# A gated state-space and feed-forward kernel: output bias seeded in PSUM, the last 64 GELU features of two token tiles multiplied in the two row halves of TensorE

## The chip, the cores and the metric

The kernel runs on one core of one Trainium2 chip. The metric is the device time of one execution in microseconds (us), less is better. Each kernel was timed several times beside the kernel before, on the same chip. All runs quoted here were classed as undisturbed ("fast"). The granted clock is the share of the full TensorE clock that the chip allowed, as the profile records it; where its mean over a run was below 0.995, the text says so.

## The reference, cut to what matters

For 2048 tokens of 640 features, a diagonal complex state-space layer (a scan over time) and a two-layer feed-forward network with 1728 hidden features read the same x and are mixed by a per-token gate.

```python
def _B_ref(x, w1, b1, w2, b2):
    h = jnp.einsum("bsd,df->bsf", x, w1) + b1
    h = _gelu(h)
    return jnp.einsum("bsf,fd->bsd", h, w2) + b2      # w2: 1728 x 640

x = A_x
g = _sigmoid((x * gate_w).sum(-1, keepdims=True))
a = _A_ref(x, ...)      # scan, then 2 Re(h C^T) + x * Dskip
b = _B_ref(x, B_w1, B_b1, B_w2, B_b2)
return g * a + (1 - g) * b
```

1728 is 13 x 128 + 64. The sum over the hidden features needs 13 matmuls of 128 rows and one of 64. In the 64-row matmul half of the TensorE array has nothing to do.

## The kernel before

The tokens are worked in 4 chunks of 512, each of 4 tiles of 128. Per chunk there are four TensorE stages: `ssm` (input projection of the scan), `ff1` (first layer and GELU), `fin_b` (second layer) and `fin_a` (output projection of the scan). In the timelines below ScalarE works in the order in which the program issues to it. The program takes all its PSUM banks from one pool of eight.

```python
def last_tile(c, p, pv):            # the last 64 hidden features, and the gate
    # ... 20 small matmuls into one bank
    nc.scalar.activation(out=gelN[c % 2][:, :, 0:F_LAST], in_=pv[:, :, 0:F_LAST], func=ACT.Gelu_apprx_tanh)
    # ... then transposed by DMA into gel[c][:, KF - 1, :]

def fold(ks):                       # folds a complex factor into C, once
    nc.scalar.activation(out=t1[:], in_=CT_im[:, ks, :], func=ACT.Identity, scale=n2im[:, ks:ks + 1])
    nc.scalar.activation(out=t2[:], in_=CT_re[:, ks, :], func=ACT.Identity, scale=n2im[:, ks:ks + 1])
    # ... two VectorE operations

def fin_b(c):
    for a in range(TPC):                                    # 4 token tiles
        # ...
        for d0, d1 in HALVES:                               # 2 x 320 output features
            p = bank()
            for kf in range(KF):                            # 14
                m = P if kf < KF - 1 else F_LAST + 1        # 128, at last 65
                nc.tensor.matmul(p[:, 0:d1 - d0], lhsT=gel[c][:m, kf, lo:lo + P], rhs=w2_sb[:m, kf, d0:d1],
                                 start=(kf == 0), stop=(kf == KF - 1))
            nc.scalar.activation(out=gb[:, d0:d1], in_=p[:, 0:d1 - d0], func=ACT.Identity, scale=gcol[:, 1, ti:ti + 1])

# order at the first chunk
ssm(1)
gates(1)
for ks in range(KS):
    fold(ks)
fin_b(0)
fin_a(0)
```

Row 65 of the last matmul is a row of ones against `b2`, so the output bias needs no instruction of its own.

Of the kernel before, what the change touches and what calls it, by code (L numbers as in the profile page):

```python
# [11 lines left out]
ACT = mybir.ActivationFunctionType  # L12
BF16 = mybir.dt.bfloat16
F32 = mybir.dt.float32
I32 = mybir.dt.int32

P = 128
T = 2048
D = 640
F = 1728  # L20
CH = 512
NCH = T // CH
KD = D // P
KS = D // P
KF = (F + P - 1) // P
F_LAST = F - (KF - 1) * P
NT = T // P
TPC = CH // P
HD = D // 2
# [9 lines left out]
def kernel(  # L39
# [19 lines left out]
    nc = tc.nc  # L59
# [4 lines left out]
    const = ctx.enter_context(tc.tile_pool(name="const", bufs=1))  # L64
# [4 lines left out]
    work = ctx.enter_context(tc.tile_pool(name="work", bufs=2))  # L69
    fwork = ctx.enter_context(tc.tile_pool(name="fwork", bufs=5))  # L70

    def bank(dtype=F32):
        return ps.tile([P, CH * 4 // (4 if dtype == F32 else 2)], dtype, name="bank")
# [7 lines left out]
    w2_sb = const.tile([P, KF, D], BF16, name="w2_sb")  # L81
# [9 lines left out]
    prmB = const.tile([NB, P], BF16, name="prmB")  # L91
    colA = const.tile([P, 3 * KS], F32, name="colA")
    colB = const.tile([P, NB], F32, name="colB")
    Dbc = const.tile([P, D], BF16, name="Dbc")
    glast = const.tile([P, 2, KS], F32, name="glast")
    carry = const.tile([P, 2, KS], F32, name="carry")
    b1x = const.tile([P, F_LAST + 1], BF16, name="b1x")
    gelN = [const.tile([P, TPC, P], BF16, name=f"gelN{i}") for i in range(2)]
    gz = const.tile([P, NT], F32, name="gz")
    gcol = const.tile([P, 2, NT], F32, name="gcol")  # L100
# [28 lines left out]
    HC = CH // 4  # L129
# [1 line left out]
    nc.gpsimd.iota(tfi[:], pattern=[[1, HC]], base=0, channel_multiplier=0)  # L131
    nc.gpsimd.memset(b1x[:, F_LAST:F_LAST + 1], 0.0)
    for i in range(2):
        nc.gpsimd.memset(gelN[i][:, :, F_LAST:P], 0.0)
        nc.gpsimd.memset(gelN[i][:, :, F_LAST:F_LAST + 1], 1.0)
    nc.scalar.dma_start(out=prmB[KS:NB, :], in_=B_b1[0:(KF - 1) * P].rearrange("(j p) -> j p", p=P))
    nc.scalar.dma_start(out=prmB[0:KS, :], in_=gate_w.rearrange("(j p) -> j p", p=P))
    nc.sync.dma_start(out=b1x[:, 0:F_LAST], in_=B_b1[F - F_LAST:F].rearrange("(o d) -> o d", o=1).to_broadcast([P, F_LAST]))  # L138
# [4 lines left out]
    nc.sync.dma_start_transpose(out=CT_im[:], in_=A_C_im[:, :])  # L143
    nc.sync.dma_start(out=w2_sb[:, 0:KF - 1, :], in_=B_w2[0:(KF - 1) * P, :].rearrange("(kf p) d -> p kf d", p=P))
    nc.sync.dma_start(out=w2_sb[:F_LAST, KF - 1, :], in_=B_w2[(KF - 1) * P:F, :])
    nc.sync.dma_start(out=w2_sb[F_LAST:F_LAST + 1, KF - 1, :], in_=B_b2.rearrange("(o d) -> o d", o=1))
    nc.sync.dma_start(out=Dbc[:], in_=A_Dskip.rearrange("(o d) -> o d", o=1).to_broadcast([P, D]))
    nc.sync.dma_start_transpose(out=xT[2][:], in_=x2d[2 * CH:3 * CH, :])
    nc.sync.dma_start_transpose(out=xT[3][:], in_=x2d[3 * CH:4 * CH, :])
# [6 lines left out]
    class Clock:  # L156
        pe = 5.0
        act = 13.0
# [23 lines left out]
    def pe(cols):  # L182
        ck.pe += cols / 2400.0 + 0.002

    def act(cost):
        ck.act = max(ck.act, ck.pe + 0.2) + cost
        return ck.act
# [18 lines left out]
    def col(name, dtype=F32, n=KS):  # L206
        return const.tile([P, n], dtype, name=name)
# [37 lines left out]
    absq = col("absq", n=NQ * KS)  # L245
    sq = col("sq", n=NQ * KS)
    cq = col("cq", n=NQ * KS)
    kk = work.tile([P, KS, HC], I32, name="bu", bufs=8)

    def over(c):  # L250
        return c.rearrange("p (k o) -> p k o", o=1).to_broadcast([P, KS, HC])
# [11 lines left out]
    gel = [None] * NCH  # L263
    gbs = [None] * NT
# [5 lines left out]
    def ff1_act(p, c, kf):  # L270
        nc.scalar.activation(out=gel[c][:, kf, :], in_=p[:, :], func=ACT.Gelu_apprx_tanh, bias=b1_c[:, kf:kf + 1])  # L271
        act(0.69)
# [5 lines left out]
    def last_bank(c):  # L278
        p = bank()
        pv = p[:, 0:TPC * NL].rearrange("p (a n) -> p a n", a=TPC)  # L280
        if c == 0:
            nc.tensor.matmul(pv, lhsT=ident[:], rhs=b1x[:].rearrange("p (o n) -> p o n", o=1).to_broadcast([P, TPC, NL]),
                             start=True, stop=True, skip_group_check=True)
            return p, pv
        nc.scalar.activation(out=pv, in_=b1x[:].rearrange("p (o n) -> p o n", o=1).to_broadcast([P, TPC, NL]), func=ACT.Identity)
        act(0.4)
        return p, pv

    def last_tile(c, p, pv):
        for a in range(TPC):  # L290
            for kd in range(KD):
                nc.tensor.matmul(p[:, a * NL:(a + 1) * NL], lhsT=xT[c][:, kd, a * P:(a + 1) * P],  # L292
                                 rhs=w1b[kd][:, n1b - NL:n1b], start=False, stop=(kd == KD - 1), skip_group_check=True)
                pe(76)
        nc.scalar.activation(out=gelN[c % 2][:, :, 0:F_LAST], in_=pv[:, :, 0:F_LAST], func=ACT.Gelu_apprx_tanh)
        act(0.45)
        nc.scalar.activation(out=gz[:, c * TPC:(c + 1) * TPC], in_=pv[:, :, F_LAST:NL].rearrange("p a o -> p (a o)"), func=ACT.Tanh, scale=0.5)
        act(0.2)
        nc.sync.dma_start_transpose(out=gel[c][:, KF - 1, :].rearrange("p (a t) -> p a t", a=TPC),
                                    in_=gelN[c % 2][:].rearrange("p a n -> p (a n)"))  # L300

    def ff1(c, k0=0):
        for kf in range(k0, KF - 1):
            p = bank()
            if kf == KF - 3:
                last = last_bank(c)
            for kd in range(KD):
                ff1_mm(p, c, kf, kd)
            ff1_act(p, c, kf)
            let_out(ck.pe)  # L310
        last_tile(c, *last)
        let_out(ck.pe)
# [38 lines left out]
    lo, hi = slice(0, HC), slice(HC, HB)  # L351
# [119 lines left out]
    def ssm(c):  # L471
        hs[c] = hsp.tile([P, 2 * KS, CH], BF16, name="hs")
        for ks in range(KS):
            bu = work.tile([P, 2, CH], BF16, name="bu", bufs=8)
            for ri, BT in enumerate((BT_re, BT_im)):
                p = bank()
                for kd in range(KD):
                    nc.tensor.matmul(p[:], lhsT=BT[:, kd, ks * P:(ks + 1) * P], rhs=xT[c][:, kd, :],  # L478
                                     start=(kd == 0), stop=(kd == KD - 1))
                    pe(CH)  # L480
                nc.scalar.activation(out=bu[:, ri, :], in_=p[:], func=ACT.Identity)  # L481
                act(0.6)
            scan_ops(c, ks, bu, ck.act)
            if c == 0 and ks == 0:
                later(0, 1.6, factors)
            let_out(ck.pe)
# [12 lines left out]
    HALVES = ((0, HD), (HD, D))  # L499
    seeded = {}  # L500

    def cuts(ti):
        return ((0, HD), (HD, 512), (512, D)) if ti == NT - 1 else HALVES

    def seed(ti):

        c, a = divmod(ti, TPC)
        seeded[ti] = []
        for d0, d1 in cuts(ti):
            p = bank()  # L510
            dve_now(ck.pe, 0.45, lambda: nc.vector.tensor_tensor(out=p[:, 0:d1 - d0], in0=xn[c][:, a, d0:d1], in1=Dbc[:, d0:d1], op=ALU.mult))  # L511
            seeded[ti].append(p)

    def fin_b(c):
        for a in range(TPC):
            ti = c * TPC + a
            lo = a * P
            gb = fwork.tile([P, D], F32, name="gb")
            if a >= TPC - 2:
                seed(c * TPC + a - (TPC - 2))  # L520
            for d0, d1 in HALVES:
                p = bank()
                for kf in range(KF):
                    m = P if kf < KF - 1 else F_LAST + 1
                    nc.tensor.matmul(p[:, 0:d1 - d0], lhsT=gel[c][:m, kf, lo:lo + P], rhs=w2_sb[:m, kf, d0:d1],  # L525
                                     start=(kf == 0), stop=(kf == KF - 1))
                    pe(d1 - d0)
                nc.scalar.activation(out=gb[:, d0:d1], in_=p[:, 0:d1 - d0], func=ACT.Identity, scale=gcol[:, 1, ti:ti + 1])  # L528
                act(0.5)
            gbs[ti] = gb  # L530
            let_out(ck.pe)

    def fin_a(c):
        for a in range(TPC):
            ti = c * TPC + a
            lo = a * P
            ot = fwork.tile([P, D], BF16, name="ot", bufs=3)
            if a < TPC - 2:
                seed(ti + 2)
            for i, (d0, d1) in enumerate(cuts(ti)):  # L540
                p = seeded[ti][i]
                for j in range(2 * KS):
                    CT = CT_re if j < KS else CT_im
                    nc.tensor.matmul(p[:, 0:d1 - d0], lhsT=hs[c][:, j, lo:lo + P], rhs=CT[:, j % KS, d0:d1],  # L544
                                     start=False, stop=(j == 2 * KS - 1), skip_group_check=True)
                    pe(d1 - d0)

                def f():
                    nc.vector.scalar_tensor_tensor(out=ot[:, d0:d1], in0=p[:, 0:d1 - d0], scalar=gcol[:, 0, ti:ti + 1],  # L549
                                                   in1=gbs[ti][:, d0:d1], op0=ALU.mult, op1=ALU.add)  # L550

                dve_now(ck.pe + 0.2, 0.45, f)
                if ti == NT - 1 and i > 0:
                    s0 = 0 if i == 1 else d0
                    q = nc.sync if i == 1 else nc.scalar
                    q.dma_start(out=out2d[ti * P:(ti + 1) * P, s0:d1], in_=ot[:, s0:d1])
            if ti < NT - 1:
                nc.sync.dma_start(out=out2d[ti * P:(ti + 1) * P, :], in_=ot[:])
# [58 lines left out]
```

## Time and profile before

218.0 us is the median of the first three runs (217.83 to 218.4).

| what | value | where it is read |
|---|---|---|
| TensorE busy | 211.9 of 216.2 us | page, part 1 |
| VectorE, ScalarE busy | 88%, 42% | page, part 1 |
| chain of waits | DMA to 22.5 us, then TensorE alone to 213.2 us | chain |
| one `fin_b` stage | 112 matmuls, 15.24 us | chain |
| one matmul over 320 columns, start to start | 136 ns for 128 rows and for 65 | single records |

Here are lines of the chain of waits of the kernel before (start in us, length in us, what ran; a piece starts where the one before it ended, which is up to 0.2 us after its first matmul started). L525 is `fin_b`, L544 `fin_a`, L478 `ssm`.

```profile
22.49 9.89 PE bank L478 x45
...
57.81 15.25 PE bank L525 x112
73.06 10.87 PE bank L544 x80
...
109.36 15.24 PE bank L525 x112
```

After 22.5 us each piece starts where the last one ended, and all are TensorE. A nanosecond saved on TensorE is saved in the time, and a wait of TensorE is lost in full.

The groups by form show the two kinds of second-layer matmul and the seed of the last first-layer bank (line, engine, operation, tiles, shapes, count; then busy us, mean ns of one, idle before).

```profile
L525 PE MATMUL bank<-w_sb,gel 128*128 128x320 bf16 x416 | 61.1, 299 | 0.0
L525 PE MATMUL bank<-w_sb,gel 65*128 65x320 bf16 x32 | 9.6, 301 | 0.0
L285 ACT ACTIVATE bank<-b1x 128x260 f32<-128x260 bf16 x3 | 1.1, 383 | 0.0
```

299 ns is the length of one pipelined matmul, not its cost: the starts are 136 ns apart. The 65-row matmul is no cheaper, so 32 x 0.136 = 4.35 us go to work that fills half the array.

The last lines are ScalarE's timeline at the first `fin_b` (an eviction is the ScalarE operation that moves a finished bank to SBUF). The first is the last eviction of `ssm`, then come the first and the last of the ten fold operations, then evictions of `fin_b`.

```profile
57.85 0.60 ACT L481 ACTIVATE bu<-bank 128x512 bf16<-128x512 f32 x1 [0.48 <-PE bank L478]
58.34 0.82 ACT L397 ACTIVATE gb<-CT_im,n2im 128x640 f32<-128x640 bf16 x1
...
64.81 0.82 ACT L399 ACTIVATE gb<-CT_re,n2im 128x640 f32<-128x640 bf16 x1
65.53 2.42 ACT L528 ACTIVATE gb<-bank,gcol 128x320 f32<-128x320 f32 x5
```

The fold holds ScalarE from 58.3 to 65.5 us, while TensorE is already in `fin_b`. Before the change this held up nothing that mattered: the first evictions only came late, there were banks enough, and the chain shows TensorE going on without a stall.

### The profile page before, as it was taken

How to read it: one execution, taken by the hardware profiler on the slowest of the kernel's cores; microseconds unless marked ns; L12 is line 12 of the kernel's file. 1: busy time of each engine (PE TensorE's matmuls, PEld its weight loads, DVE VectorE, ACT ScalarE, POOL GpSimd, SP SyncE). 2: the span in 40 equal slices, each digit the busy share in tenths (PEclk: the TensorE clock that was granted, in tenths of full speed). 3: DMA queues.
4: the chain of work that ended last, by engine and by line, in shares of the span. 5: the costliest groups of instructions: out<-in, count | busy, mean ns of one | idle time of the engine just before them, and what ended most of it. 6: DMA issues, size and time to landing. Idle time of an engine off the chain costs nothing.

```text
span 216.2 us, 3470 instructions
## 1 busy us (share of the span) xinstructions
PE 211.9 (98%) x1368; PEld 128.2 (59%) x1368; DVE 189.8 (88%) x393; ACT 91.7 (42%) x156; POOL 1.6 (1%) x12
## 2 busy tenths in 40 slices
PE   7999999999999999999999999999999999999994
PEld 3855444454577775444477777444457777777773
DVE  3889999999999899999999999999999999961152
ACT  3689456675696101556642200456662210022100
POOL 2000000000000000000000000000000000000000
PEclk9999999999999999999999999999999999999999
DMA  5999999995000042000010006100001000100011
GB/s 174 255 224 199 226 214 369 175 246 103 3 0 0 0 141 106 0 0 3 0 24 3 0 0 200 45 2 0 0 3 24 0 3 30 61 30 3 2 61 61
DMA packets 32339, 16.16 MB, mean 75 GB/s; under 512 B 25091, under 2 KB 32324, under 8 KB 32324
## 3 DMA queue, kind: packets, MB, share of 16 engines
q1 hardware_dynamic: 32114, 15.91, 30.2%
q8 instruction: 10, 0.16, 0.3%
q10 hardware_dynamic: 210, 0.04, 0.1%
q14 instruction: 5, 0.04, 0.1%
HBM read 7.24 MB, written 2.62 MB: 46 GB/s over the span
## 4 chain that ended last, share of the span: by engine, by line
PE 88%; SPq 5%; DMA 5%; issue 0%; DVE 0%
PE bank L525 28%; PE bank L544 20%; PE bank L478 20%; PE bank L267 19%; DMA BT_im<-in_A_B_im_dram 3%; SPq L139 3%; DMA xn<-in_A_x_dram 1%; SPq L127 1%; SPq L125 1%; PE bank L292 1%; SPq L124 0%; SPq L138 0%; DVE ot L549 0%
## 5 line engine op out<-in xcount | busy, mean ns | idle before, releaser
L525 PE MATMUL bank<-w_sb,gel 128*128 128x320 bf16 x448 | 61.6, 299 | 0.0
L525 PEld LDWEIGHTS <-gel 128*128 128x128 bf16 x448 | 43.6, 98 | 17.2
L481 ACT ACTIVATE bu<-bank 128x512 bf16<-128x512 f32 x40 | 23.9, 597 | 41.7 <-PE bank L478 41.7
L271 ACT ACTIVATE gel<-bank,colB 128x512 bf16<-128x512 f32 x52 | 34.6, 693 | 15.1 <-PE bank L267 14.8
L544 PEld LDWEIGHTS <-hs 128*128 128x128 bf16 x330 | 31.8, 98 | 11.9
L434 DVE TENSOR_TENSOR_SCAN g<-r_c,carry,v 128x512 bf16<-128x512 f32 x30 | 37.2, 1270 | 0.0
L528 ACT ACTIVATE gb<-bank,gcol 128x320 f32<-128x320 f32 x32 | 16.5, 527 | 48.2 <-PE bank L525 46.6
L267 PE MATMUL bank<-xT,w1b 128*128 128x512 bf16 x140 | 31.0, 379 | 0.0
L267 PE MATMUL bank<-xT,w1a 128*128 128x512 bf16 (+1 forms) x150 | 27.6, 344 | 0.0
L544 PE MATMUL bank<-CT_im,hs 128*128 128x320 bf16 (+2 forms) x165 | 27.1, 295 | 0.0
L544 PE MATMUL bank<-CT_re,hs 128*128 128x320 bf16 (+2 forms) x165 | 27.1, 295 | 0.0
L549 DVE SCALAR_TENSOR_TENSOR ot<-bank,gcol,gb 128x320 bf16<-128x320 f32 (+2 forms) x33 | 17.3, 533 | 9.5 <-PE bank L544 9.3
L478 PE MATMUL bank<-xT,BT_im 128*128 128x512 bf16 x100 | 24.9, 379 | 0.1
L478 PE MATMUL bank<-xT,BT_re 128*128 128x512 bf16 x100 | 24.8, 379 | 0.0
L267 PEld LDWEIGHTS <-w1b 128*128 128x128 bf16 x140 | 13.6, 98 | 16.3 <-DMA w1b<-in_B_w_dram 0.3
L267 PEld LDWEIGHTS <-w1a 128*128 128x128 bf16 x150 | 14.9, 100 | 11.7
L511 DVE TENSOR_TENSOR bank<-xn,Dbc 128x320 f32<-128x320 bf16 (+2 forms) x33 | 14.3, 483 | 5.8 <-ACT gb L528 5.8
L478 PEld LDWEIGHTS <-BT_im 128*128 128x128 bf16 x100 | 9.7, 98 | 12.2 <-DMA BT_im<-in_A_B_im_dram 0.6
L478 PEld LDWEIGHTS <-BT_re 128*128 128x128 bf16 x100 | 9.7, 98 | 11.0
L415 DVE TENSOR_TENSOR v<-wa,wb 128x512 bf16<-128x512 bf16 x40 | 15.2, 421 | 0.7
L415 DVE TENSOR_TENSOR wa<-TCOS,g 128x1024 bf16<-128x1024 bf16 x20 | 13.7, 686 | 0.1
L415 DVE TENSOR_TENSOR wb<-TSIN,g 128x1024 bf16<-128x1024 bf16 x20 | 13.7, 684 | 0.0
(98 smaller groups left out, 130.7 us busy)
## 6 DMA issues: line engine op xcount, KB each, us to landing
out_dram<-ot SPq DMA_DIRECT2D x15, 160.0 KB, 1.8
w_sb<-in_B_w_dram SPq DMA_DIRECT2D x1, 2080.0 KB
xn<-in_A_x_dram SPq DMA_DIRECT2D x3, 640.0 KB, 4.9
w1b<-in_B_w_dram SPq DMA_DIRECT2D x5, 240.0 KB, 4.2
w1a<-in_B_w_dram SPq DMA_DIRECT2D x5, 192.0 KB, 3.5
xn<-in_A_x_dram SPq DMA_DIRECT2D x2, 320.0 KB
Dbc<-in_A_Dskip_dram SPq DMA_DIRECT2D x1, 160.0 KB
out_dram<-ot SPq DMA_DIRECT2D x1, 128.0 KB
```

The lines of the kernel that those rows point to most:

```text
L139: nc.sync.dma_start_transpose(out=BT_re[:], in_=A_B_re[:, :])
L267: nc.tensor.matmul(p[:, t0:t1], lhsT=w, rhs=xT[c][:, kd, t0:t1], start=(kd == 0), stop=(kd == KD - 1))
L271: nc.scalar.activation(out=gel[c][:, kf, :], in_=p[:, :], func=ACT.Gelu_apprx_tanh, bias=b1_c[:, kf:kf + 1])
L415: nc.vector.tensor_tensor(out=o, in0=a, in1=b, op=op)
L434: nc.vector.tensor_tensor_scan(s["g"][:, ri, :], r_c[:, ks:ks + 1].to_broadcast([P, CH]), s["v"][:, ri, :], init, ALU.mult, ALU.add)
L478: nc.tensor.matmul(p[:], lhsT=BT[:, kd, ks * P:(ks + 1) * P], rhs=xT[c][:, kd, :], start=(kd == 0), stop=(kd == KD - 1))
L481: nc.scalar.activation(out=bu[:, ri, :], in_=p[:], func=ACT.Identity)
L511: dve_now(ck.pe, 0.45, lambda: nc.vector.tensor_tensor(out=p[:, 0:d1 - d0], in0=xn[c][:, a, d0:d1], in1=Dbc[:, d0:d1], op=ALU.mult))
L525: nc.tensor.matmul(p[:, 0:d1 - d0], lhsT=gel[c][:m, kf, lo:lo + P], rhs=w2_sb[:m, kf, d0:d1], start=(kf == 0), stop=(kf == KF - 1))
L528: nc.scalar.activation(out=gb[:, d0:d1], in_=p[:, 0:d1 - d0], func=ACT.Identity, scale=gcol[:, 1, ti:ti + 1])
L544: nc.tensor.matmul(p[:, 0:d1 - d0], lhsT=hs[c][:, j, lo:lo + P], rhs=CT[:, j % KS, d0:d1], start=False, stop=(j == 2 * KS - 1), skip_group ...
L549: nc.vector.scalar_tensor_tensor(out=ot[:, d0:d1], in0=p[:, 0:d1 - d0], scalar=gcol[:, 0, ti:ti + 1], in1=gbs[ti][:, d0:d1], op0=ALU.mult, ...
```

## The change

The intent: two tiles share the array in the last step. The 64 features of even tiles lie in rows 0 to 63, those of odd tiles in rows 64 to 127, and the last rows of `w2` are loaded into both halves. Two 64-row matmuls ("half-height" below; a group of them between full matmuls is an "excursion") can then run side by side into two banks. The row of ones no longer fits, so ScalarE writes the bias `b2` into the bank beforehand (a "seed"), and all matmuls add to it. Because a bank must be seeded before its first matmul, the seeds of tiles 0 and 1 are issued early, in the stage before, and those of tiles 2 and 3 at the start of `fin_b`. The number of `bu` buffers goes from 8 to 7 to make room for the broadcast bias.

```diff
     for i in range(2):
-        nc.gpsimd.memset(gelN[i][:, :, F_LAST:P], 0.0)
-        nc.gpsimd.memset(gelN[i][:, :, F_LAST:F_LAST + 1], 1.0)
+        nc.gpsimd.memset(gelN[i][:], 0.0)
...
-    nc.sync.dma_start(out=w2_sb[F_LAST:F_LAST + 1, KF - 1, :], in_=B_b2.rearrange("(o d) -> o d", o=1))
+    nc.sync.dma_start(out=w2_sb[F_LAST:2 * F_LAST, KF - 1, :], in_=B_w2[(KF - 1) * P:F, :])
+    nc.sync.dma_start(out=b2bc[:], in_=B_b2.rearrange("(o d) -> o d", o=1).to_broadcast([P, D]))
...
-        nc.scalar.activation(out=gelN[c % 2][:, :, 0:F_LAST], in_=pv[:, :, 0:F_LAST], func=ACT.Gelu_apprx_tanh)
+        for h in range(2):
+            nc.scalar.activation(out=gelN[c % 2][:, h::2, h * F_LAST:(h + 1) * F_LAST], in_=pv[:, h::2, 0:F_LAST], func=ACT.Gelu_apprx_tanh)
...
+            if kf == KF - 4 and c >= 2:          # in ff1
+                seed_b(c - 1, 0)
...
+            if c == 1 and ks == KS - 1:          # in ssm
+                seed_b(0, 0)
...
+    def seed_b(c, q):
+        for a in (2 * q, 2 * q + 1):
+            for i, (d0, d1) in enumerate(HALVES):
+                p = bank()
+                nc.scalar.activation(out=p[:, 0:HD], in_=b2bc[:, d0:d1], func=ACT.Identity)
+                seeded_b[c * TPC + a, i] = p
+
     def fin_b(c):
-        (the loop shown above)
+        for q in range(TPC // 2):
+            pair = (2 * q, 2 * q + 1)
+            if q == 0:
+                seed_b(c, 1)
+            for a in pair:
+                ...
+                for i, (d0, d1) in enumerate(HALVES):
+                    p = seeded_b[c * TPC + a, i]
+                    for kf in range(KF - 1):
+                        nc.tensor.matmul(p[:, 0:HD], lhsT=gel[c][:, kf, a * P:(a + 1) * P], rhs=w2_sb[:, kf, d0:d1],
+                                         start=False, stop=False, skip_group_check=True)
+            for i, (d0, d1) in enumerate(HALVES):
+                for h, a in enumerate(pair):
+                    r = slice(h * F_LAST, (h + 1) * F_LAST)
+                    nc.tensor.matmul(seeded_b[c * TPC + a, i][:, 0:HD], lhsT=gel[c][r, KF - 1, a * P:(a + 1) * P],
+                                     rhs=w2_sb[r, KF - 1, d0:d1], start=False, stop=True, skip_group_check=True)
+            for a in pair:
+                (evictions of the tile, as before)
...
+            if c == 2 and a == TPC - 1:          # in fin_a
+                seed_b(3, 0)
```

More of the change, by code (lines that the diff above doesn't have):

```diff
@@ L93 @@
     colB = const.tile([P, NB], F32, name="colB")
+    b2bc = const.tile([P, D], BF16, name="b2bc")
     Dbc = const.tile([P, D], BF16, name="Dbc")
@@ L247 @@
     cq = col("cq", n=NQ * KS)
-    kk = work.tile([P, KS, HC], I32, name="bu", bufs=8)
+    kk = work.tile([P, KS, HC], I32, name="bu", bufs=7)
     def over(c):
@@ L294, in last_tile @@
                 pe(76)
-        nc.scalar.activation(out=gelN[c % 2][:, :, 0:F_LAST], in_=pv[:, :, 0:F_LAST], func=ACT.Gelu_apprx_tanh)
-        act(0.45)
+        for h in range(2):
+            nc.scalar.activation(out=gelN[c % 2][:, h::2, h * F_LAST:(h + 1) * F_LAST], in_=pv[:, h::2, 0:F_LAST], func=ACT.Gelu_apprx_tanh)
+            act(0.3)
         nc.scalar.activation(out=gz[:, c * TPC:(c + 1) * TPC], in_=pv[:, :, F_LAST:NL].rearrange("p a o -> p (a o)"), func=ACT.Tanh, scale=0.5)
@@ L473, in ssm @@
         for ks in range(KS):
-            bu = work.tile([P, 2, CH], BF16, name="bu", bufs=8)
+            bu = work.tile([P, 2, CH], BF16, name="bu", bufs=7)
+            if c == 1 and ks == KS - 1:
+                seed_b(0, 0)
             for ri, BT in enumerate((BT_re, BT_im)):
@@ L512, in seed @@
             seeded[ti].append(p)
-    def fin_b(c):
-        for a in range(TPC):
-            ti = c * TPC + a
-            lo = a * P
-            gb = fwork.tile([P, D], F32, name="gb")
-            if a >= TPC - 2:
-                seed(c * TPC + a - (TPC - 2))
-            for d0, d1 in HALVES:
-                p = bank()
-                for kf in range(KF):
-                    m = P if kf < KF - 1 else F_LAST + 1
-                    nc.tensor.matmul(p[:, 0:d1 - d0], lhsT=gel[c][:m, kf, lo:lo + P], rhs=w2_sb[:m, kf, d0:d1],
-                                     start=(kf == 0), stop=(kf == KF - 1))
-                    pe(d1 - d0)
-                nc.scalar.activation(out=gb[:, d0:d1], in_=p[:, 0:d1 - d0], func=ACT.Identity, scale=gcol[:, 1, ti:ti + 1])
-                act(0.5)
-            gbs[ti] = gb
+    seeded_b = {}
@@ new lines, in seed_b @@
+    def seed_b(c, q):
[3 more added lines that the diff above has]
+                nc.scalar.activation(out=p[:, 0:HD], in_=b2bc[:, d0:d1], func=ACT.Identity)
+                act(0.45)
+                seeded_b[c * TPC + a, i] = p
+    def fin_b(c):
+        for q in range(TPC // 2):
[3 more added lines that the diff above has]
+            for a in pair:
+                if q == 1:
+                    seed(c * TPC + a - 2)
+                for i, (d0, d1) in enumerate(HALVES):
[3 more added lines that the diff above has]
+                                         start=False, stop=False, skip_group_check=True)
+                        pe(HD)
+            for i, (d0, d1) in enumerate(HALVES):
[3 more added lines that the diff above has]
+                                     rhs=w2_sb[r, KF - 1, d0:d1], start=False, stop=True, skip_group_check=True)
+                pe(HD)
+            for a in pair:
+                ti = c * TPC + a
+                gb = fwork.tile([P, D], F32, name="gb")
+                for i, (d0, d1) in enumerate(HALVES):
+                    nc.scalar.activation(out=gb[:, d0:d1], in_=seeded_b[ti, i][:, 0:HD], func=ACT.Identity, scale=gcol[:, 1, ti:ti + 1])
+                    act(0.5)
+                gbs[ti] = gb
```

## The prediction

> What bounds the kernel now. The page gives TensorE 211.9 of 216.2 us busy; the chain of waits is DMA and DMA issue up to 22.5 us and then TensorE alone, without a stall, to 213.2 us (L525, the second layer, 28%). So only TensorE time after 22.5 us counts, plus any new wait that reaches it. VectorE is 88% busy, ScalarE 42%; the clock is 1.00 throughout.
>
> Removed. In the chain one chunk's L525 stage is 112 matmuls in 15.24 us, 136 ns each. The 65-row last matmul also costs 136 ns, start to start; there are 32: 4.35 us. If 64-row pairs run side by side (the Trainium skill, "TensorE: Matmul & The Clock Gate", Part 3, says that matmuls in different row groups overlap; no trace here shows it yet), 16 pairs cost 2.18 us: 2.18 us saved.
>
> Added on TensorE. 8 excursions into half-height mode. The Trainium skill, "TensorEngine Tiling (Array Packing)", Key Properties, says a change of mode drains TensorE. The trace has two small-row matmuls (15 and 18 rows): the next full matmul starts 123 and 111 ns after them, where narrow matmuls otherwise follow in 29 ns. Taking 80 to 95 ns for each of 16 switches as an estimate: 1.3 to 1.5 us, and about 0.03 us per excursion for the second weight load. Net on TensorE: about -0.4 us.
>
> Moved to ScalarE. 32 seeds of 128x320: the 128x260 seed takes 383 ns, so I estimate 0.43 us each, 0.4 in a row, 13 us in all. ScalarE has room, except in two places:
> 1. The fold. In the timeline the ten fold activations (L397, L399) hold ScalarE from 58.3 to 65.5 us, and the first L525 stage starts at 57.8. The first four seeds go in before it (delaying it 0.5 us); those of tiles 2 and 3 stand behind it and land from 66.4 us. TensorE finishes tiles 0 and 1 at about 65.25 and waits about 1.2 us, once, on the critical path.
> 2. In first-layer chunks 2 and 3 four seeds (1.6 us) stand before the last GELUs (0.69 us each per 1.08 us of matmuls), so the seed of the last bank (L285) may come 0.1 to 0.2 us late: 0.3 us in all.
>
> Should not matter: evictions of two tiles together, which delay VectorE's skip seeds by under 1 us; 7 instead of 8 bu buffers (early enough in chunk 2 by about 1 us); 240 KB more DMA (DMA falls idle at 51.5 us, before the first seed); hs of the last chunk (ready at 191 us, used at 202).
>
> Sum: -2.18 + 1.6 + 1.2 + 0.3 = about +0.9 us. Predicted 218.9 us, 217.3 to 220.7 in 8 of 10 cases. Chances: faster by over 2% 0.02, within 2% 0.93, slower by over 2% 0.05.
>
> What would show it. 64-row matmuls start in pairs up to 30 ns apart, pair to pair 136 ns; gaps into and out of the group 80 to 100 ns over normal. The waits list TensorE waiting for a ScalarE seed once for over 1 us near 65 us, and short waits for L285. The L525 stages of chunks 1 and 3 are each 0.05 to 0.2 us shorter than 15.24 us. Nothing changes before 57 us.
>
> What would make it wrong. Pairs that don't overlap (about 221); a full drain of the 160 ns by which a 299 ns matmul outlasts its slot, at each switch (1.2 us more); free switches (about 217.3); ScalarE blocked by a seed whose bank VectorE frees late; or a shifted VectorE order that brings hs or the folded C of chunk 0, only about 1 us early now, too late.

## The result, and the profile after

The changed kernel took 218.77 us (median of 6 runs, 218.26 to 218.95); the kernel before 217.95 us (median of 6). The ratio is 1.0033, with a 95% interval of 1.0015 to 1.0051. Ratios here are the mean time of one kernel's fast runs over that of the other's of the same rounds, so they are not quite the ratio of the medians.

The chain of waits after (now L541 and L548 are the full and the half-height matmuls of `fin_b`, L573 is `fin_a`, L526 the bias seed):

```profile
65.19 0.61 issue
65.80 0.44 ACT bank L526
...
66.28 7.22 PE bank L541 x52
73.51 0.38 PE bank L548 x4
...
110.28 7.07 PE bank L541 x52
117.35 0.38 PE bank L548 x4
117.73 7.17 PE bank L541 x52
124.90 0.38 PE bank L548 x4
```

The chain no longer stays on TensorE: at 65.8 us it passes through a ScalarE seed, and before that through the fold. In the waits there is one new line for TensorE (who waited for whom: us in total, times, longest):

```profile
PE bank L541 <- ACT bank L526: 1.0, 1, 1.0
```

ScalarE's timeline says why. These are the first four seeds, the first and the last fold operation, the second four seeds and the evictions of tiles 0 and 1:

```profile
56.22 1.51 ACT L526 ACTIVATE bank<-b2bc 128x320 f32<-128x320 bf16 x4
...
58.61 0.83 ACT L401 ACTIVATE gb<-CT_im,n2im 128x640 f32<-128x640 bf16 x1
...
65.08 0.82 ACT L403 ACTIVATE gb<-CT_re,n2im 128x640 f32<-128x640 bf16 x1
65.80 1.51 ACT L526 ACTIVATE bank<-b2bc 128x320 f32<-128x320 bf16 x4
67.24 1.76 ACT L555 ACTIVATE gb<-bank,gcol 128x320 f32<-128x320 f32 x4
```

The groups by form, to be held against those of before:

```profile
L548 PE MATMUL bank<-w_sb,gel 64*128 64x320 bf16 x32 | 3.6, 301 | 0.0
L526 ACT ACTIVATE bank<-b2bc 128x320 f32<-128x320 bf16 x32 | 12.7, 444 | 7.7 <-DVE ot L578 7.6
```

Busy TensorE time for the last features fell from 9.6 to 3.6 us, but busy time counts overlapping matmuls once and the longer gaps around them not at all. Costs must be read from starts. In the single records of the trace, around one group of four half-height matmuls, the distances from start to start are:

| from | to | ns |
|---|---|---|
| full | full | 136 |
| last full | first half-height | 231 to 232 |
| rows 0-63 | rows 64-127 (same pair) | 3 to 4 |
| first pair | second pair | 143 |
| last half-height | next full | 228 to 229 (once 1291, at 65 us) |
| that full | the second full | 145 to 147 (136 after the long gap at 65 us) |

The pair does run side by side. From the last full matmul to the next full one it is 231.5 + 4 + 143 + 4 + 228 = 610 ns, where three plain slots would be 408 ns: 202 ns more, and 10 more in the gap after it, so an excursion into half-height mode and back costs 0.21 us. Of the 610 ns, 136 are the last full matmul's own slot, so the four half-height ones take 474 ns, with the 10 ns 484. Before, a 65-row matmul was followed after 140 ns, and the gap after that was 138 ns: 142 ns for each of the four, together 568 ns. These 6 ns go with the 65 rows and not with the end of a sum: in experiment 3, where sums end too but every matmul has 128 rows, all gaps in the `fin_b` stages of chunks 1 to 3 are 136 ns within 1 ns. So a group gains 0.08 us, and a chunk has two.

The stages give the whole account (first matmul of a stage to the first of the next, us, worked out from the records of the two profiled runs):

| | before | after | difference |
|---|---|---|---|
| all up to the first `fin_b` (57.0 to 57.8 in the 14 traces) | 57.65 | 57.68 | +0.03 |
| `fin_b`, chunk 0 | 15.25 | 16.13 | +0.88 |
| `fin_b`, chunks 1, 2, 3 | 15.25 each | 15.08 each | -0.49 in all |
| `fin_a`, four chunks | 10.87 each | 10.88 each | +0.04 in all |
| last matmul to the end | 3.27 | 3.59 | +0.32 |
| sum | | | +0.8 (span 216.2 to 217.0) |

Without its wait chunk 0 would take 15.08 us like the others, so the wait is worth 16.13 - 15.08 = 1.05 us.

### The profile page after: what moved, and what is told of

Read it like the earlier page. It is cut to its first block, busy times and chain, and to the rows that moved or that the text cites. A ratio compares the mean times of both kernels' runs of the same rounds, so it can differ in the third digit from the quotient of the medians.

```text
span 217.0 us, 3505 instructions
## 1 busy us (share of the span) xinstructions
PE 210.7 (97%) x1357; PEld 125.2 (58%) x1368; DVE 189.0 (87%) x393; ACT 100.7 (46%) x192; POOL 1.9 (1%) x10
## 4 chain that ended last, share of the span: by engine, by line
PE 72%; DVE 20%; ACT 4%; issue 1%
PE bank L541 23%; PE bank L573 20%; PE bank L268 16%; PE bank L484 10%; DVE g L438 4%; DVE wb L419 3%; DVE wa L419 2%; ACT gb L403 1%; DVE hs L419 1%; DVE v L419 1%; ACT gb L401 1%; DVE g L369 1%; PE bank L197 1%; PE bank L548 1%; DVE TCOS L370 1%
## 5 line engine op out<-in xcount | busy, mean ns | idle before, releaser
L541 PE MATMUL bank<-w_sb,gel 128*128 128x320 bf16 x416 | 57.8, 299 | 1.0 <-ACT bank L526 1.0
L541 PEld LDWEIGHTS <-gel 128*128 128x128 bf16 x416 | 40.3, 98 | 17.5 <-issue 2.0
L573 PEld LDWEIGHTS <-hs 128*128 128x128 bf16 x330 | 31.5, 98 | 12.6 <-issue 1.1
L555 ACT ACTIVATE gb<-bank,gcol 128x320 f32<-128x320 f32 x32 | 14.2, 528 | 38.0 <-PE bank L548 33.1
L573 PE MATMUL bank<-CT_re,hs 128*128 128x320 bf16 (+2 forms) x165 | 27.2, 295 | 0.0
L573 PE MATMUL bank<-CT_im,hs 128*128 128x320 bf16 (+2 forms) x165 | 27.1, 295 | 0.0
L526 ACT ACTIVATE bank<-b2bc 128x320 f32<-128x320 bf16 x32 | 12.7, 444 | 7.7 <-DVE ot L578 7.6
```

What stands on the lines that cost most here:

```text
L526: nc.scalar.activation(out=p[:, 0:HD], in_=b2bc[:, d0:d1], func=ACT.Identity)
L541: nc.tensor.matmul(p[:, 0:HD], lhsT=gel[c][:, kf, a * P:(a + 1) * P], rhs=w2_sb[:, kf, d0:d1], start=False, stop=False, skip_group_check=True)
L555: nc.scalar.activation(out=gb[:, d0:d1], in_=seeded_b[ti, i][:, 0:HD], func=ACT.Identity, scale=gcol[:, 1, ti:ti + 1])
L573: nc.tensor.matmul(p[:, 0:d1 - d0], lhsT=hs[c][:, j, lo:lo + P], rhs=CT[:, j % KS, d0:d1], start=False, stop=(j == 2 * KS - 1), skip_group ...
```

## The experiments

Theory 1: the half-height pairs gain a little on TensorE, overlap less mode changes, and one wait for a seed that stands behind the fold on ScalarE gives more than that back. Rival A: the mode changes eat the gain by themselves. Rival B: seeds, longer held banks or the missing `bu` buffer slow things generally. There were ten kernels, on three chips, with the kernel before beside them; all gave correct results. The changed kernel was beside them only in experiments 2, 9 and 11; elsewhere stages are the safer measure. The edits are against the changed kernel unless said otherwise.

### 1 and 2. The late seeds moved into the fold

```diff
     for ks in range(KS):
+        if ks == KS - 2:
+            seed_b(0, 1)
         fold(ks)
...
-            if q == 0:
+            if q == 0 and c > 0:
                 seed_b(c, 1)
```

> The seeds of tiles 2 and 3 of chunk 0 are issued after the third of the five folds instead of after the last, nothing else changes. Theory 1 (the loss is one 1.06 us wait of TensorE for a ScalarE seed behind the fold): the 1291 ns gap at 65 us becomes the normal 228 ns, the chunk-0 second-layer stage falls from 16.13 to about 15.08 us, the time from 218.8 to about 217.7 us, a little under before. Rival A (the mode switches eat the gain): the wait is hidden behind something else and the time stays at 218.8. Rival B (seeds and held banks press on everything): about 218.8, with a new wait elsewhere, for instance for the folded C, which now comes 1.05 us later.

Measured: 217.94 us, with runs from 217.1 to 218.47; before in the same rounds 217.99; ratio 1.0002 (0.9974 to 1.0029). The wait is gone. ScalarE's timeline of this run (the sixth fold operation, the seeds, the seventh), then its chain:

```profile
61.57 0.82 ACT L403 ACTIVATE gb<-CT_re,n2im 128x640 f32<-128x640 bf16 x1
62.29 1.50 ACT L526 ACTIVATE bank<-b2bc 128x320 f32<-128x320 bf16 x4
63.73 0.82 ACT L401 ACTIVATE gb<-CT_im,n2im 128x640 f32<-128x640 bf16 x1
```

```profile
57.20 7.06 PE bank L541 x52
64.27 0.38 PE bank L548 x4
64.65 7.17 PE bank L541 x52
```

The seeds land from 62.7 us, TensorE comes to tiles 2 and 3 at about 64.6 us, and the stage of chunk 0 takes 15.08 us like the others. The folded C, now later, is still early enough for `fin_a` (ready at 68.9 us, used at 72.1). Because the runs scattered, the kernel ran again beside the changed kernel:

> The changed kernel as it is, so that the next runs have it in their own rounds: 218.8 us within 0.3, 0.8 us over before, the 1.29 us gap at 65 us again.

> The same kernel as in the first run of this study, whose rounds scattered by 1.4 us: beside the changed kernel on one chip. By the stages of the trace it should be 1.05 us under the changed kernel and 0.6 us under before: 217.3 to 217.8.

Measured: the changed kernel 218.75 us (ratio 1.0044, 1.0022 to 1.0065), this one 217.55 us (0.9991, 0.9973 to 1.0009), before 217.77 us. Moving four ScalarE instructions is worth 1.2 us of medians, 1.05 us by the stages. Theory 1 holds, Rival A falls as the explanation of the loss. But with the wait gone the change still brings nothing that is clear of noise.

### 3. No half-height mode: full rows with zeros

```diff
-                    r = slice(h * F_LAST, (h + 1) * F_LAST)
+                    r = slice(0, P)
```

> Everything of the change stays (seeds, pairs of tiles, order) but the last matmul of each tile uses all 128 rows, of which the other tile's 64 hold zeros; the result stays right. No mode switch, no overlap. Theory 1 (a pair group gains 0.08 us net: overlap 0.27 less two switches of about 0.09): stages of chunks 1 to 3 return from 15.08 to 15.25 us; time about 0.55 us over the changed kernel, 219.3. Rival A (the half-height mode loses): faster than the changed kernel.

Measured: 218.73 us, ratio to before 1.0036 (1.0012 to 1.0059); the `fin_b` stages of chunks 1 to 3 took 15.21 us against 15.08 for the changed kernel, and the wait in chunk 0 shrank (a gap of 1128 ns), as the seeds come at a fixed moment. The stages say what was expected but for the gaps of 140 and 138 ns, which are gone with the 65-row matmuls (15.21 instead of 15.25). The expected time, 219.3 us, did not come: 218.73 against 218.77 is no difference. One reason shows in the traces: the DMA-bound start up to the first `fin_b` took 57.05 us here and 57.68 us in the changed kernel. The net gain of the half-height groups, 0.13 us in each of chunks 1 to 3, is visible in the trace and too small for this timing.

### 4. The seeds alone, without half-height mode and without the wait

This is the edit of experiment 1 and that of experiment 3 together.

> All 128 rows in the last matmul (no half-height mode) and the seeds of tiles 2 and 3 of chunk 0 moved into the fold: what is left of the change is seeding the output bias from ScalarE, evicting two tiles together, and 7 bu buffers. Theory 1: free once placed, 217.95 as before, within 0.3. Rival B (seeds, held banks, later evictions cost of themselves): clearly over before, by 0.5 us or more.

Measured: 217.86 us against 217.79 before, ratio 1.0009 (0.9995 to 1.0023). The 32 seeds (12.7 us of ScalarE in the changed kernel) cost nothing that the timing resolves once the four late ones are placed well: at most 0.23% or 0.5 us by the interval, and all four `fin_b` stages take 15.21 to 15.22 us. What is left of Rival B is the 0.32 us at the end of the program (see below), which this run has too.

### 5. The kernel before with 7 `bu` buffers

```diff
-            bu = work.tile([P, 2, CH], BF16, name="bu", bufs=8)
+            bu = work.tile([P, 2, CH], BF16, name="bu", bufs=7)
```

(The edit is against the kernel before, and the scratch tile of the same name is edited likewise.)

> The kernel before with 7 instead of 8 bu buffers, nothing else. Theory 1: no change (218.0 within 0.2); ScalarE may wait for VectorE once in chunk 2, TensorE does not. Rival B: slower by some tenths of a us.

Measured: 217.90 us, ratio 1.0008 (0.9997 to 1.0020); every stage after the DMA-bound start is the same to 0.01 us. The buffer does not matter.

### 6. Both tiles in the same row half

```diff
-            nc.scalar.activation(out=gelN[c % 2][:, h::2, h * F_LAST:(h + 1) * F_LAST], ...)
+            nc.scalar.activation(out=gelN[c % 2][:, h::2, 0:F_LAST], ...)
...
-                    r = slice(h * F_LAST, (h + 1) * F_LAST)
+                    r = slice(0, F_LAST)
```

> Half-height mode and its switches stay, but both tiles of a pair use rows 0 to 63, so nothing can run side by side; the result stays right. Theory 1 (the pair really overlaps): the 4 ns between the two matmuls of a pair become about 136, each of 16 pairs costs 0.13 us more; stages of chunks 1 to 3 rise from 15.08 to about 15.6 us; about 1.85 us over the changed kernel (2.1 less 0.26 that the stall of chunk 0 hides), 220.6. If the side by side start were only a matter of the record and the array did the work one after the other: no change.

Measured: 220.14 us, ratio to before 1.0114 (1.0101 to 1.0127). Stages of chunks 1 to 3: 15.62 us. The distance within a pair is 135 to 136 ns instead of 3 to 4. The group by form shows the same as busy time:

```profile
L548 PE MATMUL bank<-w_sb,gel 64*128 64x320 bf16 x32 | 5.7, 299 | 0.0
```

5.7 us against 3.6 with two halves. The overlap is real, it needs different row halves, and it is worth 0.54 us a chunk.

### 7. Twice as many excursions

```diff
+                    if a == pair[1]:     # after the 13 full matmuls of half i
+                        for h, b in enumerate(pair):
+                            (the two half-height matmuls of half i)
```

> Each pair of half-height matmuls is an excursion of its own: four per chunk instead of two. Theory 1: about 0.19 us for each of 8 more excursions, stages of chunks 1 to 3 about 15.47 us; about 1.4 us over the changed kernel, 220.2 (one of the eight hides in the stall). With the joined run this gives three points, 1, 2 and 4 excursions a chunk.

Measured: 219.96 us, ratio to before 1.0108 (1.0091 to 1.0124); stages of chunks 1 to 3 took 15.51 us. Two more excursions a chunk cost 0.43 us.

### 8. One excursion a chunk

The banks are seeded, so the sum can be done in any order: the half-height matmuls of tiles 2 and 3 can come first in their sums, right after those of tiles 0 and 1, which come last in theirs.

```diff
+    def halves(c, q):
+        (the half-height matmuls of pair q; stop=(q == 0))
...
-            (the half-height matmuls of this pair)
+            if q == 0:
+                halves(c, 0)
+                halves(c, 1)
```

> The half-height matmuls of tiles 2 and 3 come right after those of tiles 0 and 1, so that a chunk has one excursion into half-height mode instead of two; the banks are seeded, so the order of the sum is free. Theory 1 with two switches of about 0.1 us per excursion: stages of chunks 1 to 3 fall from 15.08 to about 14.89 us, chunk 0 by about 0.1; time about 0.7 us under the changed kernel, 218.1. If the cost is not in the switches but in each pair: no change.

Measured: 219.42 us (218.42 to 220.16), ratio 1.0063 (1.0031 to 1.0095): slower than the changed kernel, a miss. The stages of chunks 1 to 3 did what was expected, 14.88 us. Chunk 0 did not: 18.61 us. The windows of its trace (stretch, length, TensorE busy, granted clock, DMA share, GB/s) show two things:

```profile
65.00:66.00 1.00, 0.29 (x1) 1.00 0.00 0
66.00:67.00 1.00, 0.65 (x3) 0.85 0.00 0
67.00:68.00 1.00, 1.00 (x5) 0.50 0.00 0
...
70.00:71.00 1.00, 1.00 (x9) 0.94 0.00 0
```

First, the expectation forgot that a joined group needs all four late seeds before it can leave, not only the first. The gaps in the group were 1295, 719 and 354 ns, so TensorE had nothing to do for (1295 - 136) + (719 - 136) + (354 - 136) = 1960 ns, against 1291 - 136 = 1155 ns in the changed kernel. Second, the granted clock fell to 0.50 from 66.71 to 70.12 us, that is for 3.41 us, with the matmuls 267 ns apart. Three of the six runs had a mean clock of 0.989 to 0.991 (219.73 to 220.16 us), the other three 0.997 to 0.998 (218.42 to 219.10 us).

### 9. The wait doubled

To see whether that fall belongs to the joined group or to the wait, the four late seeds were each written twice in the changed kernel.

```diff
+        if c == 0 and q == 1:
+            for a in (2, 3):
+                for i, (d0, d1) in enumerate(HALVES):
+                    nc.scalar.activation(out=seeded_b[a, i][:, 0:HD], in_=b2bc[:, d0:d1], func=ACT.Identity)
```

> The four late seeds of chunk 0 are each written twice, so they land 1.45 us later; the result stays right. Theory 1: the gap of 1.29 us becomes about 2.7 us and the time rises by the same 1.45 us, to 220.2 us: a wait of TensorE there costs its full length. The joined run without the moved seeds showed more: with about 2.3 us of waiting in one 3.41 us stretch the granted clock fell to 0.5 for the next 3.41 us in three of its six runs. If that holds for any wait of this length, some or all runs here lose about 1.7 us more (mean clock about 0.99, near 221.9); if it needs the half-height mode, none does.

Measured: 221.65 us (219.73 to 222.11), ratio 1.0164 (1.0134 to 1.0193). The gap became 2730 ns. Five of six runs had a mean clock of 0.989 to 0.992 (221.3 to 222.11 us); the sixth had 1.0 and took 219.73 us. The windows of the profiled run:

```profile
67.00:68.00 1.00, 0.68 (x4) 0.72 0.00 0
68.00:69.00 1.00, 1.00 (x5) 0.50 0.00 0
```

Its chunk-0 stage took 19.25 us. That is 16.13 of the changed kernel, plus 1.44 for the longer gap, plus 1.70 for 3.41 us at half clock, which together are 19.27. The fall needs neither the joined group nor a wait in pieces. That it needs no half-height mode, as the expectation meant to test, is not shown: here too half-height matmuls come right before the wait, and no run has a wait of this length without them. So a wait of 2.5 us cost its length and in five of six runs about 1.7 us more; with the 1.06 us of the changed kernel the fall was seen in none of 12 runs.

The traces show one more thing. In all 14 of them every stretch at full clock that ended was a whole multiple of 3.413 us long (before both falls 61.44 us, 18 times; in the changed kernel 211.63 us, 62 times), and each of the two falls took one such step. So the clock changed on a grid of fixed steps here. That a wait escapes when it happens to be split over two steps would explain why not every run fell; it is not shown, as no run of these two kernels that escaped was traced.

### 10 and 11. Both edits: seeds in the fold, one excursion a chunk

> Both edits of the two runs above that move the seeds into the fold and join the excursions. If stall and switches are separate costs they add: about 1.06 + 0.8 = 1.85 us under the changed kernel, 216.9 us, about 1.0 us under before. Rival B: less than the sum.

Measured: 216.57 us (216.45 to 216.67), before 217.99, ratio 0.9936 (0.9914 to 0.9959). Once more, beside the changed kernel:

> The version with seeds in the fold and one excursion a chunk, once more beside the changed kernel: 216.6 us within 0.3, about 2.2 us under the changed kernel, 1.3 us under before; no run with a lowered clock.

Measured: 216.56 us (216.27 to 216.80), before 217.77, changed kernel 218.75; ratio to before 0.9942 (0.9928 to 0.9956). No run had a clock below 0.998. The chain of the second of these runs, in chunk 1 (L549 full, L534 half-height):

```profile
108.74 7.06 PE bank L549 x52
115.80 0.65 PE bank L534 x8
116.45 7.17 PE bank L549 x52
```

All four `fin_b` stages take 14.88 us, chunk 0 too. This version beats both kernels: 1.2 to 1.4 us under before, 2.2 us under the change.

### The excursions together

`fin_b` stage of chunks 1 to 3, mean of three, from the runs above:

| excursions a chunk | side by side | us |
|---|---|---|
| 0 (experiment 3) | no | 15.21 |
| 1 (experiments 8, 10) | yes | 14.88 |
| 2 (the change) | yes | 15.08 |
| 2 (experiment 6) | no | 15.62 |
| 4 (experiment 7) | yes | 15.51 |

Each excursion costs 0.20 to 0.21 us, and the line through 1, 2 and 4 meets zero excursions near 14.67 us. So the overlap alone is worth about 15.21 - 14.67 = 0.54 us a chunk, as experiment 6 says directly (15.62 - 15.08).

## Why the prediction was right

It said 218.9 us and the time was 218.77 us. The terms, in us for the whole kernel:

| term | predicted | measured |
|---|---|---|
| matmul time saved by pairs | -2.18 | -2.15 (4 x 0.54) |
| 8 excursions | +1.3 to 1.5 and 0.24 | +1.7 (8 x 0.21) |
| gaps of 140 and 138 ns gone | not named | -0.13 (4 x 0.03) |
| wait for the seed behind the fold | +1.2 | +1.05 |
| late seed of the last first-layer bank | +0.3 | 0 |
| end of the program | not named | +0.32 |
| start, up to the first `fin_b` | 0 | +0.03 (scatter) |

- What bounds the kernel was right: everything that came or went was TensorE time on the chain, except the end of the program.
- The pairs overlap, as the Trainium skill says ("TensorE: Matmul & The Clock Gate", Part 3, which gives about 4 ns between starts); the trace has 3 to 4 ns, and experiment 6 shows that without different halves the gain is gone.
- The cost of a mode change was estimated from two small matmuls in the trace of before, which the next full one followed after 111 and 123 ns instead of 29. The real changes lengthen their gaps by 95 and 92 ns. That estimate decided the prediction: counting only the saved slots would have said -2.18 us. That these two could stand for a change to 64 rows was a guess, and partly luck: the 65-row matmuls of the same trace lengthen the next two gaps by only 4 and 2 ns.
- The wait behind the fold was predicted at its place and nearly in its size, from the order of issue and from durations alone. It was a little shorter than predicted because the first four seeds put the fold off by 0.27 us and not by 0.5 us: the late seeds landed from 66.23 us, not 66.4.
- Of the rivals named in the prediction, two did not come: no full 160 ns drain per change, no late hs. A third, a ScalarE blocked by banks that VectorE frees late, did come, from 178 to 189 us: seeds waited seven times, 7.6 us in all (the idle time in the seeds' group line above). It cost nothing, as the last seed landed at 189.54 us and TensorE came to its tile pair at 195.0 us. The `bu` buffer was rightly left out (experiment 5).

The prediction's second wait was the step that was wrong. The prediction put it as the seed of the last first-layer bank coming "0.1 to 0.2 us late: 0.3 us in all". The four seeds before the last GELUs took 1.51 us (not 1.6), and the last bank's seed was just in time. In ScalarE's timeline after the change:

```profile
107.06 1.51 ACT L526 ACTIVATE bank<-b2bc 128x320 f32<-128x320 bf16 x4
...
109.07 0.39 ACT L286 ACTIVATE bank<-b1x 128x260 f32<-128x260 bf16 x1
```

It ends at 109.46 us, the matmuls that add to it start at 109.51 us, and that stage is as long as before (0.61 us). In the next chunk the same seed ends at 160.85 us, and its matmuls start at 160.91 us. The term was a difference of two near-equal numbers.

The end of the program was not in the prediction at all. From the start of the last matmul to the last record it takes 3.59 to 3.61 us in every traced run with the change in it (the changed kernel and experiments 1 to 4 and 6 to 11) and 3.27 to 3.28 us in the kernel before and in experiment 5. The last output's landing is not what grew: counted from the start of the last matmul, SyncE's waits for outputs end at 2.26 us in the changed kernel and at 2.35 us in the kernel before. After them SyncE goes on at 2.74 us instead of 2.40 us, and the closing exchange of all engines follows that much later. The cause stays open. This +0.32 us and the wrong +0.3 us cancel, so the sum is closer than its parts.

## What to carry to other kernels

A new instruction on an engine with much idle time is free only if nothing long stands before it in that engine's order at the moment when the busy engine needs it: look at the timeline at that moment, not at the busy share. Packing two half-height matmuls pays one slot a pair (0.136 us here) and costs two mode changes a visit (0.21 us here), so with one pair a visit it loses (15.51 against 15.21 us a stage). Collect them in as few visits as the order of the sum allows; seeded sums can be done in any order. When something new waits for several results, count the last of them, and remember that a wait of a few microseconds can also cost clock, as in experiments 8 and 9.

## What the Trainium skill lacked or had wrong

- "TensorEngine Tiling (Array Packing)", Key Properties, says that changing the tiling mode drains TensorE and gives no cost. Here a visit to half-height mode and back costs 0.21 us: a gap of 231 ns going in, 228 ns coming out and 146 ns after that where 136 is normal, and 0.20 to 0.21 us per visit from stages with 1, 2 and 4 visits.
- The same page gives row tiling of two as a speedup of up to 2x. For 64-row matmuls over 320 columns in groups of four, the overlap was worth 0.54 us a chunk and the two visits took 0.41 us of it (stage 15.21 to 15.08 us); with one visit a chunk more was left (15.21 to 14.88 us). How many small matmuls share a visit decides the gain, and the page does not say so.
- "TensorE: Matmul & The Clock Gate", "Why this matters for your kernels", advises no gaps over about 3 us between matmul bursts. Here the clock fell to 0.5 for one 3.41 us stretch already after 1.96 us without work in three pieces (3 of 6 runs) and after one gap of 2.73 us from start to start (5 of 6 runs), not after a gap of 1.29 us (0 of 12); the counts are by the runs' mean clock, and one run of each kernel was traced (two of the last). The 3.41 us length of the stretch agrees with the window of 3413 ns in Part 1 of that page. Which part of the stretch before must be idle was not measured.
- No page has the 6 ns that a 65-row matmul adds to the two gaps after it (140 and 138 instead of 136 ns; with 128 rows in its place they are gone), nor anything that explains the 0.32 us at the end of the program.
